# Two FNet and attention layers on one core: a PSUM bank closed to early maxima, an earlier root, query low parts on VectorE, and maxima paced by deadlines

## The chip, the cores and the metric

The kernel runs on one core of one Trainium2 chip. The metric is the device time of one execution in microseconds (us), the median of several runs. The core's engines work side by side and wait for each other by semaphores: TensorE (PE in the profile; its weight loads are PEld), VectorE (DVE), ScalarE (ACT), GpSimd (POOL), and SyncE (SP), which here only issues DMAs. PE writes its results into PSUM, which has eight banks of 128 partitions x 512 fp32 numbers.

## The reference, cut to what matters

Two different sublayers follow each other twice, on x of 2048 tokens x 512 features:

```
x = x + Real(DFT_seq(DFT_hidden(layernorm(x))))         # A: matrix products with cos and sin
x = x + softmax(q k^T / 4) v @ wo, of layernorm(x)      # B: 32 heads of 16, one k and one v for all heads
```

All of it is fp32. Layer norm has no weights; its epsilon is 1e-5. q is layernorm(x) @ wq, and k and v, 16 columns each, are shared by the heads.

## The kernel before

**Numbers in two parts.** Where one fp32r product would not be precise enough, an operand is split into a high part (rounded to fp32r) and a low part (what is left), and a product is made of three matmuls (`mm3`, lines 86 to 89). So most steps of preparation are a copy to the high part on ScalarE and a subtraction for the low part on VectorE or GpSimd (`split_ps`, `split_sb`, `split_act`, lines 70 to 84).

**Two layers, two phases each.** `phase_a` (line 733) makes the Fourier sublayer and the queries, keys and values; `phase_b` (line 1132) makes the attention and its output projection. Tokens are 16 tiles of 128, in four blocks (`tb`) of four tiles.

**Phase A** is a loop over n = 0 to 127: four blocks x (cosine, sine) x 16 tiles of the sequence. One n multiplies one 128x512 piece of the sequence matrix (loaded as `craw`, split into `ch` and `cl`) with the normalised input (`xnh`, `xnl`). From n = 48 on, `z_rows` (line 800) runs two matmuls at a time, on the upper and lower 64 rows of the array, and takes two pieces together. After each block, the hidden matrix follows (`y_tile`, `y_rows`), the residual is added and stored to `mid` by a DMA from GpSimd's queue, and the tile gets its layer norm: statistics on VectorE (`ln_stats`), the square root on ScalarE and the variance plus epsilon on GpSimd (`ln_root`, line 146), a reciprocal and four small operations (`ln_inv`, line 153), and the normalisation itself, in place (`ln_apply`, line 190). Then it is transposed on PE into PSUM bank z and split (`tr_tile`, line 263); from it come keys and values (`kv`) and queries (`q_mm`, `q_half`, `q_rows`). Query parts go to DRAM (`q_store`, `q_half_store`), 6 DMAs on SP for each group of heads.

**Maxima.** The softmax needs the maximum of each row of scores before phase B exponentiates it. For each unit (query tile, pair of heads, half of the array, quarter of the keys), PE multiplies queries and keys into a PSUM bank and VectorE reduces 512 numbers to their maximum. Some of these (`EARLY`, lines 35 to 40) run in phase A, between other matmuls: `pump` (line 445) offers a turn after each pair of matmuls, and `issue` (line 453) takes it if a bank is free by the planner's own clocks (`clk`: it adds 0.6 us to VectorE for each maximum, and keeps the times at which the three y banks and the one z bank come free). It picks bank z if that is free no later than the next y bank, and if `hold` isn't set. The others are listed in `units` (line 945), 1472 a layer, and run in phase B.

**PSUM.** Three banks y and one bank z, one at a time by turns, and two pairs x of two banks. Bank z serves the transposes (line 266), the early maxima, and in phase B the sum of the attention.

**The tail of phase A.** The last block's tiles 12 to 15 come late, and each is handled on its own. Tiles 12 and 13 are finished at n = 119; then, at the end of the n named, root of both (119), `ln_inv` (120), normalisation of 12 (121), transposes of 12 and normalisation of 13 (122), transposes of 13 (123), keys and values of both (124). After the loop (lines 915 to 942) an order written out by hand follows: `y_tile` of 14 and 15, transposes of 14 (`tr(14)`), the first two query groups of tiles 12 and 13 (`q_half(12, 0)`, `q_half(12, 1)`) with the root of tile 15 between them, their stores, the third group, `tr(15)`, the fourth, keys and values of 14 and 15, the queries of 14 and 15 by `q_rows`, the last maxima of tile 0, the row maxima written into the query tile (`max_rows_pe`, line 547), and six units as a lead for phase B. `q_split` (line 366) copies a query group twice on ScalarE (`raw`, then the high part), and GpSimd subtracts for the low part; for groups 2 and 3 of tiles 14 and 15 this is deferred (`st["subs"]`) to after `max_rows_pe`. `raw` is one tile, used for groups 0 and 1 and again for 2 and 3.

**Phase B** is a loop over n = 0 to 511: 16 query tiles x 32 steps. A step has four score matmuls (`score`, line 963), exponentials of 128x1024 on ScalarE, four matmuls with the values (`pv`, line 987) for the step two before, and maxima of later query tiles (`more_max`), up to two after the second score and two after the fourth. How many is set by `owed`:

```
return min(3 * (n + 1) + 6, len(units)) - o.done
```

A query tile's maxima must be done 8 steps before it starts (`max_neg_a`, with an assertion at lines 1177 to 1181; the two halves of the last two tiles have dates of their own). The order of the two halves of the array in a step follows the unit that is next (`g`, line 1148).

Of the kernel before, what the change touches and what calls it, by code (L numbers as in the profile page):

```python
# [22 lines left out]
NT = S // P  # L23
# [6 lines left out]
NSTEP = 32  # L30
# [17 lines left out]
def fnet_mqa_kernel(ctx: ExitStack, tc: tile.TileContext, x_in, ct, dt_, wq, wkv, wo, out):  # L48
# [6 lines left out]
    def f(ap):  # L55
        return ap.bitcast(F32)
# [139 lines left out]
    def make_layer(L, src, mid, dst, last):  # L196
# [169 lines left out]
        def q_split(t0, g, pq):  # L366
            if g == 0:
                st["raw"] = half(6)
                if t0 == 14:
                    st["stage"] = slot(3, F32R)  # L370
            hl = half((4, 5, 0, 1)[g], F32R) if t0 == 12 else st["stage"][:, g * 512:(g + 1) * 512]
            raw = st["raw"][:, 256 * (g % 2):256 * (g % 2) + 256]
            nc.scalar.copy(raw, pq)
            nc.scalar.copy(hl[:, :256], raw)
            st["qs", t0, g] = hl
            sub = lambda: nc.gpsimd.tensor_sub(hl[:, 256:], raw, f(hl[:, :256]))
            (st["subs"].append(sub) if t0 == 14 and g > 1 else sub())

        def q_half_store(t0, g):
            hl = st["qs", t0, g]  # L380
# [352 lines left out]
        def phase_a(extra):  # L733
# [111 lines left out]
            add(120, lambda: ln_inv(*st["root"]))  # L845
            add(121, lambda: apply(12))
            add(122, lambda: (tr(12), apply(13)))
            add(123, lambda: tr(13))
            add(124, kv_early)
            for k in ((125, 1), (125, 3), (126, 0), (126, 1), (126, 3), (127, 0), (127, 1), (127, 3)):  # L850
                inner[k] = [lambda: take(ma, 1)]
# [2 lines left out]
            for n in range(128):  # L854
# [47 lines left out]
                if n % 32 == 31 and tb < 3:  # L902
# [5 lines left out]
                    for k, v in prep_tasks(tb, dict(x1)).items():  # L908
                        for fn in v:
                            if isinstance(k, tuple):  # L910
                                inner.setdefault(k, []).append(fn)
                            else:
# [5 lines left out]
            y_tile(3, 3, zh, zl, x1[3], {2: [lambda: root(14, 1)], 4: [lambda: ln_inv(*st["root"], nc.vector)],  # L918
                                         6: [lambda: apply(14)]})
            tr(14)  # L920
            q_half(12, 0, *xt[0])
            root(15, 1)
            ln_inv(*st["root"], nc.vector)
            apply(15)
            q_half(12, 1, *xt[0])
            q_half_store(12, 0)
            q_half(12, 2, *xt[0])
            q_half_store(12, 1)
# [7 lines left out]
            take(mb, 99)  # L936
            max_neg(0, 0, HALF, 5)
            max_rows_pe(0, 0, HALF)
            for sub in st["subs"]:
                sub()  # L940
            for k in range(6):
                more_max()

# [8 lines left out]
                max_half(*units[o.done])  # L952
                o.done += 1

        def owed(n):
            return min(3 * (n + 1) + 6, len(units)) - o.done

        def done_with(i, pr):
            return all(u[:2] > (i, pr) for u in units[o.done:])
# [172 lines left out]
        def phase_b(nxt):  # L1132
            nonlocal woh, wol, osp
            woh = slot(4, F32R).rearrange("p (k e) -> p k e", k=NK)
            wol = slot(5, F32R).rearrange("p (k e) -> p k e", k=NK)
            def wo_load(j):
                st["wo", j] = half(4 + j)
                nc.sync.dma_start(st["wo", j], wo[:, j, :])

            behind = []  # L1140
            for n in range(NT * NSTEP):
                i, s_ = divmod(n, NSTEP)
                if len(behind) == 2:
                    pv(*behind.pop(0))
                behind.append((i, s_))
                if i > 0 and s_ == 13:
                    o_proj(i - 1)
                g = units[o.done][2] if o.done < len(units) else 1
                for j, m in ((g, 0), (1 - g, 2), (2 + g, 0), (3 - g, 2)):
                    score(i, s_, j)  # L1150
                    for _ in range(m):
                        if owed(n) >= 1:
                            more_max()
                if n in (1, 3):
                    q_half_store(12, 2 + n // 2)
                if i == 0 and 17 <= s_ <= 23 and s_ % 2:
                    q_half_store(14, s_ // 2 - 8)
                if 12 <= n < 16:
                    wo_load(n - 12)
                if n == 25:  # L1160
                    osp = slot(3, F32R).rearrange("p (a h n) -> p a h n", a=2, h=2)
                if i == 0 and s_ in (20, 22, 24, 26):
                    j = s_ // 2 - 10
                    split_sb(st["wo", j], woh[:, j, :], wol[:, j, :], nc.gpsimd)
                if i > 0:
                    for fn in out_tasks(i - 1).get(s_, ()):
                        fn()
                for j in range(2, NT):
                    if i == (j // 4 if j < 5 else j - 4 if j < 13 else j - 2):
                        at = {2: 11, 3: 27, 4: 6}.get(j, 0)  # L1170
                        if s_ == at:
                            qT_load(j)
                        if s_ == at + 4:
                            o.loaded.add(j)
                for fn in half_tasks(i).get(s_, ()):
                    fn()
                for at, j, p0, np_ in ((NT - AHEAD, i, HALF, HALF), (NSTEP - AHEAD, i + 1, 0, HALF if i >= NT - 3 else NPAIR)):
                    if j in (0, NT - 2, NT - 1) or j == i + 1 < NT:
                        if s_ == at:
                            assert done_with(j, p0 + np_ - 1)  # L1180
                            max_neg_a(j, p0, np_)
                        if s_ == at + 1:
                            max_neg_b(np_)
                        if s_ == at + 2:
                            max_rows(j, p0, np_)
            if nxt is not None:
                nxt.a_start()
            for at in behind:
                pv(*at)
            return {**out_tasks(NT - 1), 12: [lambda: o_proj(NT - 1)]}  # L1190
# [65 lines left out]
```

## Time and profile before

| | us |
|---|---|
| median of 3 runs | 3546.07 (3544.29 to 3546.45) |
| the profiled execution | 3549.72 |
| its span, first to last instruction | 3547.9 |
| PE busy | 3505.9 (99%) |
| DVE busy | 2714.7 (77%) |
| ACT busy | 2503.3 (71%) |
| POOL busy | 830.5 (23%) |

The profile is of one execution. A line of its timeline has a start and a duration in us, the engine, the line of the kernel, the operation, the names of the tiles written and read, shapes, how many instructions were merged into it (x2), and in brackets the idle time of the engine before it and what ended it. A line of a group has busy time and mean ns of one, then idle time. A line of the windows view has the stretch and its length, the busy time of PE, PEld, DVE, ACT and POOL (each with its count of instructions), then the clock granted to PE as a share of the full one, the share of DMA, and GB/s. Matmuls are pipelined, so a matmul's duration is longer than the time from one to the next. Layer 0 starts phase B near 632 us, layer 1 near 2393 us.

### The profile page before, as it was taken

How to read it: one execution, taken by the hardware profiler on the slowest of the kernel's cores; microseconds unless marked ns; L12 is line 12 of the kernel's file. 1: busy time of each engine (PE TensorE's matmuls, PEld its weight loads, DVE VectorE, ACT ScalarE, POOL GpSimd, SP SyncE). 2: the span in 40 equal slices, each digit the busy share in tenths (PEclk: the TensorE clock that was granted, in tenths of full speed). 3: DMA queues.
4: the chain of work that ended last, by engine and by line, in shares of the span. 5: the costliest groups of instructions: out<-in, count | busy, mean ns of one | idle time of the engine just before them, and what ended most of it. 6: DMA issues, size and time to landing. Idle time of an engine off the chain costs nothing.

```text
span 3547.9 us, 64282 instructions
## 1 busy us (share of the span) xinstructions
PE 3505.9 (99%) x24576; PEld 1874.8 (53%) x24576; DVE 2714.7 (77%) x4892; ACT 2503.3 (71%) x3210; POOL 830.5 (23%) x1262
## 2 busy tenths in 40 slices
PE   8999999999999999999999999999999999999999
PEld 6887878433333333333378878883333333333333
DVE  6267776888888888888432777768888888888883
ACT  4223733888888888888932247438888888888888
POOL 4244342211221122112213443422101110111011
PEclk9999999999999999999999999999999999999999
DMA  6435252311111100111144342523111111011100
GB/s 191 150 144 167 80 165 87 85 56 34 35 35 51 36 23 23 49 34 26 40 137 128 127 150 90 153 66 88 47 37 35 49 34 38 23 35 37 37 23 25
DMA packets 224900, 254.55 MB, mean 72 GB/s; under 512 B 52880, under 2 KB 174800, under 8 KB 217424
## 3 DMA queue, kind: packets, MB, share of 16 engines
q1 hardware_dynamic: 210384, 233.12, 21.6%
q0 software_dynamic: 14208, 17.33, 1.6%
q8 instruction: 193, 3.16, 0.4%
q14 instruction: 115, 0.94, 0.1%
HBM read 187.16 MB, written 65.27 MB: 71 GB/s over the span
## 4 chain that ended last, share of the span: by engine, by line
PE 91%; issue 2%; DVE 2%; ACT 2%; POOL 1%; DMA 1%; SPq 0%; ACTq 0%; POOLq 0%; DVEq 0%
PE z L994 29%; PE x L980 19%; PE y L408 13%; PE x L809 11%; PE y L87 3%; PE y L88 3%; PE y L89 2%; PE y L475 2%; PE x L87 2%; PE x L89 2%; PE x L88 2%; PE x L593 1%; PE z L475 1%; DVE row L191 1%; POOL cl L79 1%
## 5 line engine op out<-in xcount | busy, mean ns | idle before, releaser
L983 ACT ACTIVATE slot<-x 128x1024 f32<-128x1024 f32 x2000 | 1945.9, 1024 | 284.5 <-PE x L980 276.2
L409 DVE TENSOR_REDUCE mxp<-y 128x1 f32<-128x512 f32 x2944 | 1849.6, 684 | 181.5 <-PE y L408 168.7
L994 PE MATMUL z<-slot,v 128*32 128x512 f32 x8192 | 1096.3, 605 | 1.6 <-DVE lnv L1105 0.7
L980 PE MATMUL x<-slot,kz 64*128 64x512 f32 x2976 | 677.3, 450 | 2.2 <-DMA slot<-craw 1.7
L980 PEld LDWEIGHTS x<-slot,kz 64*128 64x128 f32 x2976 | 279.2, 184 | 744.7 <-ACT slot L983 685.8
L408 PE MATMUL y<-kz,slot 64*128 64x512 f32 x2176 | 581.6, 397 | 1.9 <-DVE mxp L409 1.9
L809 PE MATMUL x<-cl,xnh 64*128 64x512 f32 (+1 forms) x1536 | 355.8, 357 | 0.0
L994 PEld LDWEIGHTS z<-slot,v 128*32 128x32 f32 x8192 | 163.4, 108 | 363.7 <-issue 332.8
L809 PE MATMUL x<-ch,xnh 64*128 64x512 f32 (+1 forms) x1536 | 348.1, 361 | 2.3 <-ACT row L796 2.2
L809 PE MATMUL x<-ch,xnl 64*128 64x512 f32 (+1 forms) x1536 | 346.2, 362 | 0.9 <-ACT xnl L580 0.9
L408 PEld LDWEIGHTS y<-kz,slot 64*128 64x128 f32 x2176 | 276.7, 186 | 22.8 <-DVE mxp L409 10.8
L79 POOL TENSOR_TENSOR cl<-craw,ch 128x512 fp32r<-128x512 f32 x176 | 223.9, 1295 | 225.5 <-ACT ch L78 174.3
L78 ACT CAST ch<-craw 128x512 fp32r<-128x512 f32 x256 | 154.6, 622 | 170.9 <-PE x L89 87.1
L475 PE MATMUL y<-kz,slot 64*128 64x512 f32 x690 | 271.7, 405 | 2.1 <-ACT rel L479 1.2
L543 POOL DMA_DIRECT2D slot<-mt x224 | 112.1, 508 | 585.2 <-PE y L408 490.1
L809 PEld LDWEIGHTS x<-ch,xnh 64*128 64x128 f32 x1536 | 213.1, 188 | 23.3 <-issue 5.2
L809 PEld LDWEIGHTS x<-cl,xnh 64*128 64x128 f32 x1536 | 217.7, 188 | 12.6
L489 DVE TENSOR_REDUCE mxe<-y 128x1 f32<-128x512 f32 x316 | 198.8, 679 | 29.3 <-PE y L475 28.7
L809 PEld LDWEIGHTS x<-ch,xnl 64*128 64x128 f32 x1536 | 209.7, 187 | 21.1 <-issue 5.9
L1035 POOL TENSOR_TENSOR row<-row,row 128x256 f32<-128x256 f32 x63 | 46.5, 738 | 700.3 <-DMA row<-rd 654.0
L87 PE MATMUL x<-ch,xnh 128*128 128x512 f32 x384 | 154.3, 402 | 9.1 <-ACT ch L78 8.4
L89 PE MATMUL x<-ch,xnl 128*128 128x512 f32 x384 | 153.4, 399 | 2.6 <-POOL xnl L659 2.6
(198 smaller groups left out, 4143.3 us busy)
## 6 DMA issues: line engine op xcount, KB each, us to landing
craw<-ct_in SPq DMA_DIRECT2D x112, 512.0 KB
slot<-qd SPq DMA_DIRECT2D x44, 1024.0 KB
qd<-row SPq DMA_DIRECT2D x144, 128.0 KB
od<-row SPq DMA_DIRECT2D x252, 64.0 KB
row<-wqd SPq DMA_DIRECT2D x48, 256.0 KB
row<-x_in SPq DMA_DIRECT2D x32, 256.0 KB
mid<-row POOLq DMA_DIRECT2D x32, 256.0 KB, 2.4
craw<-ct_in SPq DMA_DIRECT2D x32, 256.0 KB
```

Of the source, the lines that this page charges most:

```text
L79: (eng or nc.vector).tensor_sub(lo, raw, f(hi))
L87: nc.tensor.matmul(ps_, ah, bh, start=start, stop=False)
L88: nc.tensor.matmul(ps_, ah, bl, start=False, stop=False)
L89: nc.tensor.matmul(ps_, al, bh, start=False, stop=stop)
L408: nc.tensor.matmul(pm, o.qT[i][gs, pr, :], kz[gs, c0:c0 + n], start=True, stop=True)
L409: nc.vector.reduce_max(to, pm, axis=AX.X)
L475: nc.tensor.matmul(pm, o.qT[i][gs, pr, :], k[gs, c0:c0 + 512], start=True, stop=True)
L489: nc.vector.reduce_max(to, pm, axis=AX.X)
L809: nc.tensor.matmul(z[d], a[gs, s, d * P:(d + 1) * P], b[gs, :], start=first and q < 2 and e == 0, stop=last and q > 1 and e == len(turns) - 1)
L980: nc.tensor.matmul(st["e"][:, g, :], kz[64 * g:64 * g + KR, c * P:(c + 1) * P], o.qT[i][64 * g:64 * g + KR, cp:cp + 4, :], start=True, sto ...
L983: nc.scalar.activation(ptiles[i, s_][:, 2 * w:2 * w + 2, :], st.pop("e"), AF.Exp, scale=DH ** -0.5)
L994: nc.tensor.matmul(a[32 * j:32 * j + 32, :], v1[:, c, :], pt[:, j, :], start=c == 0, stop=c == NT - 1)
```

## The change

Four edits, all in the order of work; no arithmetic is changed.

1. **Bank z closed to maxima.** `hold` is set after the second quarter of n = 122, that is ahead of the transposes of tile 12, and released behind those of tile 13. In between, early maxima use y banks only.
2. **The last tile's root sooner.** `root(15, 1)` stands ahead of `q_half(12, 0)` instead of behind it.
3. **First query low parts by VectorE.** The subtractions for groups 0 and 1 of tiles 12 and 13 are deferred and run on VectorE (`lows(2)`), behind `q_half(12, 1)` and tile 15's normalisation, ahead of the first store. The deferred ones of tiles 14 and 15 stay on GpSimd where they were.
4. **Maxima per step by deadlines.** `owed` gives way to `share`: each date at which a set of units must be done is a goal; a step gets the largest of (units still missing) / (steps left) over the goals, at least 2, with the fraction carried over, at most 4.

```diff
-            sub = lambda: nc.gpsimd.tensor_sub(hl[:, 256:], raw, f(hl[:, :256]))
-            (st["subs"].append(sub) if t0 == 14 and g > 1 else sub())
+            sub = lambda eng=nc.gpsimd: eng.tensor_sub(hl[:, 256:], raw, f(hl[:, :256]))
+            (st["subs"].append(sub) if (t0 == 14) == (g > 1) else sub())
+
+        def lows(n, eng=nc.vector):
+            for _ in range(n):
+                st["subs"].pop(0)(eng)
...
-            add(123, lambda: tr(13))
+            add(123, lambda: (tr(13), st.update(hold=False)))
+            inner[122, 1] = [lambda: st.update(hold=True)]
...
             tr(14)
+            root(15, 1)
             q_half(12, 0, *xt[0])
-            root(15, 1)
             ln_inv(*st["root"], nc.vector)
             apply(15)
             q_half(12, 1, *xt[0])
+            lows(2)
             q_half_store(12, 0)
...
-            for sub in st["subs"]:
-                sub()
+            lows(2, nc.gpsimd)
...
-        def owed(n):
-            return min(3 * (n + 1) + 6, len(units)) - o.done
+        goals = []
+        for j in range(NT):
+            for lim in (HALF, NPAIR):
+                at = NSTEP * (j - 1) + NSTEP - AHEAD if j < NT - 2 or lim == HALF else NSTEP * j + NT - AHEAD
+                if j == 0:
+                    at = NT - AHEAD
+                goals.append((sum(u[0] < j or (u[0] == j and u[1] < lim) for u in units), at))
+
+        def share(n):
+            need = max((c - o.done) / max(1, at - n) for c, at in goals if at > n or c > o.done)
+            st["due"] = min(st.get("due", 0.0) + max(2.0, need), 4.0)
+            k = int(st["due"])
+            st["due"] -= k
+            return k
...
+                left = share(n) if o.done < len(units) else 0
                 for j, m in ((g, 0), (1 - g, 2), (2 + g, 0), (3 - g, 2)):
                     score(i, s_, j)
                     for _ in range(m):
-                        if owed(n) >= 1:
+                        if left:
                             more_max()
+                            left -= 1
```

## The prediction

> **What bounds the kernel now.** I read the chain that ended last first, then the timeline of each engine at the places where TensorE (PE) is idle or slow, then the granted clock around them.
>
> ```profile
> PE 91%; issue 2%; DVE 2%; ACT 2%; POOL 1%; DMA 1%; SPq 0%; ACTq 0%; POOLq 0%; DVEq 0%
> ```
>
> PE makes up 91% of the chain. So a change pays where PE stands idle, or where it runs at less than its full clock; other engines' time counts only where PE waits for it. The longest stage is phase B (512 steps in each layer). Its maxima on VectorE (DVE) show its beat, here in layer 1:
>
> ```profile
> 2408.70 1.89 DVE L409 TENSOR_REDUCE mxp<-y 128x1 f32<-128x512 f32 x3 [0.24 <-PE y L408]
> 2410.84 1.89 DVE L409 TENSOR_REDUCE mxp<-y 128x1 f32<-128x512 f32 x3 [0.24 <-PE y L408]
> 2412.96 1.89 DVE L409 TENSOR_REDUCE mxp<-y 128x1 f32<-128x512 f32 x3 [0.24 <-PE y L408]
> ```
>
> Three maxima a step, a step each 2.12 to 2.14 us (from start to start), and DVE waits 0.24 us of each for PE. The end of phase A is where PE stops. Its own timeline, first layer 0, then the same place in layer 1:
>
> ```profile
> 582.32 0.50 PE L475 MATMUL z<-kz,slot 64*128 64x512 f32 x1
> ...
> 583.37 0.49 PE L475 MATMUL y<-kz,slot 64*128 64x512 f32 x1
> ...
> 584.51 0.30 PE L809 MATMUL x<-ch,xnl 64*128 64x256 f32 x2
> 584.63 0.30 PE L809 MATMUL x<-cl,xnh 64*128 64x256 f32 x2
> ...
> 584.77 0.48 PE L809 MATMUL x<-ch,xnh 64*128 64x256 f32 x2
> 586.96 0.66 PE L268 MATMUL z<-ident,row 128*128 128x128 f32 x4 [1.70 <-DVE mxp L489]
> ```
>
> ```profile
> 2347.97 0.66 PE L268 MATMUL z<-ident,row 128*128 128x128 f32 x4 [1.71 <-DVE mxp L489]
> ```
>
> The transposes of tile 13 (L268) want bank z, and wait 1.7 us in each layer for a maximum that was put into that bank ahead of them. DVE at that time:
>
> ```profile
> 581.57 0.69 DVE L75 TENSOR_TENSOR xnl<-z,xnh 128x512 fp32r<-128x512 f32 x1 [0.65 <-ACT xnh L71]
> ...
> 582.63 1.28 DVE L489 TENSOR_REDUCE mxp<-y 128x1 f32<-128x512 f32 x2
> 583.83 0.68 DVE L489 TENSOR_REDUCE mxp<-z 128x1 f32<-128x512 f32 x1
> 584.43 1.88 DVE L489 TENSOR_REDUCE mxp<-y 128x1 f32<-128x512 f32 x3
> 586.22 0.68 DVE L489 TENSOR_REDUCE mxp<-z 128x1 f32<-128x512 f32 x1
> ```
>
> Seven maxima are served one after another, 0.6 us each; the last, in z, ends at 586.90. What follows is worse than it looks. In the windows view the column that counts is PEclk, the granted clock:
>
> ```profile
> 584.50:587.90 3.40, 1.70 (x20) 1.21 (x18) 2.40 (x5) 0.25 (x1) 0.00 (x0) 1.00 0.00 0
> 587.90:591.40 3.50, 3.50 (x36) 3.50 (x34) 1.89 (x3) 1.57 (x4) 2.52 (x2) 0.51 0.02 5
> ...
> 2349.20:2352.60 3.40, 3.40 (x36) 3.40 (x34) 1.89 (x3) 1.28 (x4) 2.52 (x2) 0.50 0.00 0
> 301.20:304.60 3.40, 2.42 (x16) 1.34 (x14) 2.55 (x5) 1.21 (x4) 0.09 (x1) 1.00 0.00 0
> 304.60:308.00 3.40, 3.40 (x10) 2.62 (x9) 1.69 (x3) 0.00 (x0) 0.00 (x0) 0.50 0.00 0
> 2062.50:2065.90 3.40, 2.43 (x12) 1.77 (x13) 2.72 (x5) 1.09 (x4) 0.00 (x0) 1.00 0.02 5
> 2065.90:2069.30 3.40, 3.40 (x25) 2.54 (x25) 1.77 (x4) 1.22 (x2) 0.50 (x1) 1.00 0.33 93
> ```
>
> Behind the stall PE runs 3.4 us at half clock, in both layers. The matmul pairs there:
>
> ```profile
> 588.25 0.42 PE L809 MATMUL x<-ch,xnl 64*128 64x256 f32 x2
> 588.47 0.42 PE L809 MATMUL x<-ch,xnh 64*128 64x256 f32 x2
> ```
>
> From one pair to the next it is 0.22 us; from 584.51 to 584.63 it was 0.12. At half clock 3.4 us do the work of about 1.85: the dip costs some 1.55 us, which is to say nearly as much as the stall itself.
>
> **The change, part by part.** *Bank z closed (hold), each layer.* No operation is added or removed: the planner puts the maxima between the two tiles' transposes into the three y banks alone. Gone is the wait at 586.96 (1.70). Gone too is a wait of 0.2 us at 582.32, where the first of these z maxima waited for the DVE subtraction that read z until 582.26. What is late next is a y bank: the max at 583.37 reuses the bank of the first one, whose reduction ended just before, at 583.3. With hold it would come one max sooner in the order but at the same planner time, that is 0.2 us ahead of that reduction, as the wait at z no longer delays it: 0.2 us given back. From there DVE serves one in 0.6 us and the planner counts 0.6 (line 431), so no bank is later than planned. Net 1.70, between 0.85 (half of it returns as waits at y) and 1.85 (from 586.96 back to 585.11, one pair behind the last). One max slides behind tile 13's transposes; there PE has the same work, and DVE was idle for it. Tile 13's subtraction is needed only by the key matmul, 24 pairs or 2.8 us later.
>
> *The dip.* Without the stall, PE has no idle time here that could bring the dip on: 1.55 more, or nothing if something else causes it. As the windows need not lie alike in every execution (0.98 us of idle time brought a dip at 304.60 and 0.97 none at 2065.90), I count nine in ten: 1.4.
>
> The Trainium skill, "TensorE: Matmul & The Clock Gate" (Part 1: The HAM clock gate), says that the array clock halves by a free-running window of 3413 ns and, under HAM oscillation, warns of idle gaps above some 3.4 us. The dips' length here agrees (3.4 us in the windows view). By the gap length that it names, 1.7 us is too short to be the cause, and the sum would lose the 1.4. The dip at 304.60, behind 0.98 us of idle time, speaks against that reading.
>
> *Last tile's root sooner, low parts by VectorE, each layer.* The rows of tile 15:
>
> ```profile
> 616.62 0.37 ACT L373 COPY row<-x 128x256 f32<-128x256 f32 x1 [0.82 <-PE x L89]
> ...
> 617.33 0.29 ACT L149 ACTIVATE lnw<-mv,eps 128x1 f32<-128x1 f32 x1
> ...
> 619.90 0.41 ACT L374 CAST row<-row 128x256 fp32r<-128x256 f32 x1
> 620.75 0.60 ACT L71 ACTIVATE xnh<-z 128x512 fp32r<-128x512 f32 x1 [0.44 <-PE z L268]
> ```
>
> ```profile
> 615.75 0.60 POOL L577 DMA_DIRECT2D mid<-row  x1 [4.48 <-DVE row L576]
> 617.51 0.73 POOL L376 TENSOR_TENSOR row<-row,row 128x256 fp32r<-128x256 f32 x1 [1.16 <-ACT row L374]
> ```
>
> ```profile
> 616.22 0.18 DVE L144 BATCH_NORM_AGGREGATE mv<-bst 128x2 f32<-128x6 f32 x1
> ...
> 617.85 0.41 DVE L157 TENSOR_TENSOR lnw<-rs 128x1 f32<-128x1 f32 x1
> ...
> 619.05 0.88 DVE L191 TENSOR_SCALAR row<-row,mv,rs 128x512 f32<-128x512 f32 x1
> ...
> L73 DVE SCALAR_TENSOR_TENSOR slot<-x,slot 128x256 fp32r<-128x256 f32 x16 | 6.7, 420 | 4.4 <-ACT slot L71 4.4
> ```
>
> ```profile
> 620.08 0.63 PE L268 MATMUL z<-ident,row 128*128 128x128 f32 x4 [0.68 <-DVE row L191]
> ...
> 622.12 0.38 PE L88 MATMUL y<-xnl,wkvh 128*128 128x256 f32 x1
> ```
>
> The root stood behind the first query copies on ScalarE (616.62 to 617.4) and its chain beside a GpSimd subtraction, which stretched L157 to 0.41 us. Moved ahead, it starts when the variance is there (L144, 616.40), and with 0.29 for the root, tile 14's subtraction before it on DVE until 617.0 and five small DVE operations of 0.2 each (L157 has 0.41 only beside GpSimd) it ends near 618.0. The normalisation (L191) writes in place, so it must also wait until the store issued by GpSimd at 615.75 has landed; the page's section 6 has 2.4 us for these:
>
> ```profile
> mid<-row POOLq DMA_DIRECT2D x32, 256.0 KB, 2.4
> ```
>
> So L191 starts near 618.2 and, at 0.55 to 0.88, ends at 619.1 at the latest, and PE, done with the matmuls ahead at 619.2, can transpose then instead of at 620.08: 0.84 us. Not all of it lasts. ScalarE must still finish L374 (619.90 + 0.41), so tile 15's high part ends near 620.85 instead of 621.35, its low part 0.5 us sooner than before, and the key matmul that reads it (622.12) starts at 621.58: net 0.54. The two low parts on DVE (a subtraction of 128x256, which the trace does not show on DVE from SBUF alone; between the 0.42 of L73, as wide, and the 0.69 of L75, twice as wide; I take 0.42) lie between L191 and tile 15's own subtraction near 620.85, where DVE is otherwise idle. At 0.69, and with L191 ending last, the first would end at 619.8, and the ScalarE copy that overwrites its raw part, due at 619.5 (ahead of the L374 at 619.90), would wait 0.3 us. Queued behind the first of their stores on SP are the other query stores, nothing else for long:
>
> ```profile
> 617.45 7.86 SPq L385 DMA_DIRECT2D qd<-row  x12
> 633.93 1.58 SPq L556 DMA_DIRECT2D slot<-craw  x2
> ```
>
> The stores end 8.6 us before SP's next turn, so 1 us later costs nothing. The term: 0.54, between 0.2 (that wait, or GpSimd's next subtraction stretching tile 15's low part by 0.33 as the one at 617.51 did L157 and the one after it L191) and 0.84.
>
> *Maxima per step by deadlines.* There are 1472 units in a layer, 6 done beforehand. Before, three a step until step 488. The deadlines ask (1472 - 6) / 488 = 3.004 a step, the tightest of all (the next, step 408, asks 2.97); the loads keep ahead of both. Worked through, it is three in every step but 192 and 379, which get four, and none after 487. DVE needs 4 x 0.63 = 2.5 us for such a step, 0.4 over the beat, and makes it good in two steps of 0.24 idle: I cost it at nothing, at most 4 x 0.4 = 1.6 in all.
>
> *Sum.* 1.70 + 1.40 + 0.54 = 3.64 a layer, 7.3 in all. The profiled execution took 3549.72 us (span 3547.9), 3.65 above the median; the same 7.3 taken from the median 3546.07 gives **3538.8**. A measurement of this kernel can tell about 0.2%, 7.1 us, from no change: the forecast lies on that line (3539.0).
>
> **The rivals.** *The wait moves to the y banks.* Three banks for seven maxima instead of four; for it, the max at 583.37 already found its bank free only just in time; against it, DVE and planner keep one pace. Half the stall returns: 2 x (0.85 + 0.54) = 2.8 with the dip kept, 5.6 without: 3540.5 to 3543.3.
>
> *The dip is not the stall's.* For it, 2062.50 lost as much as 301.20 without a dip; against it, both layers have it right behind the stall. 2 x (1.70 + 0.54) = 4.5: 3541.6. The Trainium skill's page, read by its gap length, would have it so.
>
> *A dip fewer elsewhere*, as everything shifts against the windows: 1.6 less, 3537.2.
>
> *The change does not do it*: something else ends the wait, and only the root counts, 1.1: 3545.0. The row names the maximum, so this is small.
>
> *Slower.* Place: phase B. The extra max at step 192 swaps which half of the array each step starts with, until 379: 187 steps a layer, 374 in all. It decides from 7.3 / 374 = 0.02 us a step; at 0.05 it costs 18.7, and gives 3557.5. Against it, successive steps already start with opposite halves, and the rows above lie 2.14 and 2.12 apart.
>
> **How the numbers follow.** Forecast (3537.4 to 3540.4): 0.62, of which 0.47 lies below 3539.0. Wait moved to y: 0.17. Dip not the stall's: 0.08. A dip fewer elsewhere: 0.06. Without effect: 0.03. Slower: 0.04, of which 0.01 stays within 0.2%. Faster by over 0.2%: 0.47 + 0.06 = 0.53; slower 0.03; the rest, 0.44, within. The range 3536.5 to 3543.0 holds the forecast, the dip rivals and nearly all of the y-bank case, over 0.8.
>
> **What would show it.** Right: no idle time above 0.3 us before the L268 of tile 13, all maxima between the two tiles in y, a granted clock of 1.00 behind it in both layers, L268 of tile 15 without a wait, the phase B beat unchanged at 2.13. Wrong: PE idle before L475 on y by DVE L489; a dip that stays; a beat above 2.15 between steps 192 and 379; ScalarE late at tile 15 by the low parts.

## The result and the profile after

| | before | after |
|---|---|---|
| median of 22 runs each (range), us | 3547.39 (3544.29 to 3550.55) | 3542.59 (3540.58 to 3544.26) |
| ratio, 95% interval | | 0.9986 (0.998 to 0.9991) |
| profiled execution, us (span) | 3549.72 (3547.9) | 3541.5 (3539.7) |

The kernel is faster by about 4.8 us, between 3.2 and 7.1 us by the interval. That lies within the 0.2% named in the prediction, for which it gave the smaller chance (0.44). The forecast was 3538.8 and 7.3 us of gain, so two thirds of the gain came. The time lies in the wide range of 3536.5 to 3543.0, but not in the forecast's own part of it, 3537.4 to 3540.4. It lies where the prediction put two of its rivals (3540.5 to 3543.3 and 3541.6), so it is the traces that have to tell them apart. The kernel before was itself 1.3 us slower in these runs than the 3546.07 that the forecast started from.

The chain that ended last, from the page of the kernel after, has PE at 93% where it had 91%:

```profile
PE 93%; DVE 2%; ACT 2%; issue 2%; POOL 1%; DMA 1%; SPq 0%; ACTq 0%; DVEq 0%; POOLq 0%
```

PE's timeline of the kernel after, at the end of phase A, layer 0 and then layer 1 (start, us, engine, line, operation; a wait would stand in brackets at the end):

```profile
578.10 0.66 PE L268 MATMUL z<-ident,row 128*128 128x128 f32 x4
...
580.29 0.39 PE L479 MATMUL y<-kz,slot 64*128 64x512 f32 x1
...
582.60 0.40 PE L479 MATMUL y<-kz,slot 64*128 64x512 f32 x1
582.92 0.66 PE L268 MATMUL z<-ident,row 128*128 128x128 f32 x4
...
2336.13 0.66 PE L268 MATMUL z<-ident,row 128*128 128x128 f32 x4
2340.95 0.66 PE L268 MATMUL z<-ident,row 128*128 128x128 f32 x4
```

Six maxima stand between the two tiles, where seven stood, all of them in y, and the transposes of tile 13 start without a wait, 4.82 us behind those of tile 12 in both layers. The same distance was 6.71 us (580.25 to 586.96). The granted clock around it, from the windows view of the kernel after (stretch; length, PE, PEld, DVE, ACT, POOL busy; PEclk; DMA share; GB/s):

```profile
579.80:583.20 3.40, 3.33 (x44) 2.88 (x41) 3.40 (x7) 0.00 (x0) 0.00 (x0) 1.00 0.01 2
583.20:586.60 3.40, 3.40 (x53) 3.23 (x52) 3.31 (x6) 1.82 (x4) 1.80 (x2) 1.00 0.02 5
2341.30:2344.70 3.40, 3.40 (x53) 3.23 (x52) 3.31 (x6) 1.82 (x4) 1.87 (x2) 1.00 0.00 0
```

PE is busy nearly throughout (3.33 us of the first 3.40) and the clock is 1.00 in both layers: stall and dip are gone. DVE is now busy nearly all the time as well, up to 3.40 of 3.40 us.

**Tile 15** came out differently in the two layers. VectorE, ScalarE and PE of the kernel after, first layer 0 and then layer 1:

```profile
613.51 0.55 DVE L191 TENSOR_SCALAR row<-row,mv,rs 128x512 f32<-128x512 f32 x1 [0.97 <-DMA mid<-row]
613.97 0.75 DVE L376 TENSOR_TENSOR row<-row,row 128x256 fp32r<-128x256 f32 x2
...
2370.92 0.55 DVE L191 TENSOR_SCALAR row<-row,mv,rs 128x512 f32<-128x512 f32 x1 [0.36 <-DMA mid<-row]
2371.38 0.76 DVE L376 TENSOR_TENSOR row<-row,row 128x256 fp32r<-128x256 f32 x2
```

```profile
614.48 0.37 ACT L373 COPY row<-x 128x256 f32<-128x256 f32 x1 [0.99 <-DVE row L376]
...
2372.13 0.37 ACT L373 COPY row<-x 128x256 f32<-128x256 f32 x1 [0.60 <-PE x L89]
```

```profile
609.21 0.60 PE L268 MATMUL z<-ident,row 128*128 128x128 f32 x4
614.20 0.63 PE L268 MATMUL z<-ident,row 128*128 128x128 f32 x4
635.16 1.93 PE L1011 MATMUL z<-slot,v 128*32 128x512 f32 x8
...
2367.24 0.60 PE L268 MATMUL z<-ident,row 128*128 128x128 f32 x4
2392.79 1.93 PE L1011 MATMUL z<-slot,v 128*32 128x512 f32 x8
```

Tile 15's normalisation (L191) no longer waits for the root but for the store of the row that it overwrites, 0.97 us in layer 0 and 0.36 in layer 1. The two low parts (L376) stand behind it. In layer 0 the third query copy on ScalarE (L373) therefore waits for a low part; in layer 1 it waits for PE, as it should. The transposes of tile 15 come 4.99 us behind those of tile 14 in layer 0 and 4.68 in layer 1; before it was 5.52 in both. From tile 14's transposes to the first matmul with values it is now 25.95 and 25.55 us, where it was 26.16 and 26.12: 0.21 and 0.57 gained. The two ends of that way in the kernel before, layer 0:

```profile
614.56 0.60 PE L268 MATMUL z<-ident,row 128*128 128x128 f32 x4
640.72 1.93 PE L994 MATMUL z<-slot,v 128*32 128x512 f32 x8
```

The way also depends on when the half clock at the start of phase B sets in. In layer 1 of the run of edit 1 it set in later than usual, and the way was 25.83 us without any edit to tile 15.

### The profile page after: what moved, and what is told of

It is laid out like the page before. It is cut to its first block, busy times and chain, and to the rows that moved or that the text cites. A ratio compares the mean times of both kernels' runs of the same rounds, so it can differ in the third digit from the quotient of the medians.

```text
span 3539.7 us, 64288 instructions
## 1 busy us (share of the span) xinstructions
PE 3502.0 (99%) x24576; PEld 1870.9 (53%) x24576; DVE 2713.8 (77%) x4896; ACT 2502.3 (71%) x3210; POOL 825.9 (23%) x1258
## 4 chain that ended last, share of the span: by engine, by line
PE 93%; DVE 2%; ACT 2%; issue 2%; POOL 1%; DMA 1%; SPq 0%; ACTq 0%; DVEq 0%; POOLq 0%
PE z L1011 29%; PE x L997 19%; PE y L412 13%; PE x L813 11%; PE y L87 3%; PE y L479 3%; PE y L88 3%; PE y L89 2%; PE x L87 2%; PE x L89 2%; PE x L88 2%; PE x L597 2%; PE z L479 1%; DVE row L191 1%; POOL cl L79 0%
```

## The experiments

The theory at the start: hold, and the dip that goes with the stall, make the gain, and the shortfall against 7.3 us is a dip that the stall does not bring on in every execution (theory A in the quoted texts; A' and A'' are its versions for tile 15 and for the pacing). The rival, theory B: hold and dip are worth what was forecast, the dip in nine of ten, and root, low parts or the new pacing give some back. A third reading is that the stall has nothing to do with the dip. Four runs take the change apart; the rest follow their leads, and the theory of the dip was changed on the way. Each expectation is quoted as it was written before its run.

**Edit 1 alone.** `hold` in the kernel before:

```diff
-            add(123, lambda: tr(13))
+            add(123, lambda: (tr(13), st.update(hold=False)))
+            inner[122, 1] = [lambda: st.update(hold=True)]
```

> Edit 1 alone (bank z closed to maxima between the transposes of tiles 12 and 13). Theory A (stall always, half-clock dip only in executions whose clock window holds most of the stall, about one in two): 1.8 us of stall in each layer, and 1.57 in half of the cases: 5.2 us faster than before. Theory B (the recorded forecast: dip in nine of ten): 2 x (1.7 + 1.4) = 6.2 faster. If the wait only moved to the y banks: under 3 us faster. In the trace: no idle time above 0.3 us before L268 of tile 13, six maxima between the two tiles' transposes instead of seven.

Measured: 3542.36 us against 3547.18 for the kernel before, ratio 0.9988 (0.9979 to 0.9997). Tile 13 follows tile 12 after 4.82 us in both layers, with six maxima between them, and there is no dip. The gain of 4.3 us (1.1 to 7.5) is about that of the whole change; it does not part the expected 5.2 from 6.2, nor from less than 3.

**The stall kept, its idle time filled.** Seven matmuls whose result is not used stand ahead of tile 13's transposes in the kernel before:

```diff
+            def fill():
+                pm = bank("y")
+                for _ in range(7):
+                    nc.tensor.matmul(pm, o.qT[0][:, 0, :], kz[:, :512], start=True, stop=True)
-            add(123, lambda: tr(13))
+            add(123, lambda: (fill(), tr(13)))
```

> Kernel before with seven full-array matmuls (0.23 us each, into a free y bank, their result not used) put ahead of tile 13's transposes: TensorE still cannot start those before the maximum in bank z is done, but it is not idle meanwhile. If the dip is the stall's: granted clock 1.00 behind it in both layers, while L268 of tile 13 stays near 586.9 after an unshifted start. Time: theory A 1.6 us faster than before (two layers, one in two), theory B 2.8 faster. If the dip is not caused by the idle time: the dip stays and the time is that of before.

PE's timeline in this kernel, then its windows, layer 0 and layer 1:

```profile
585.61 1.90 PE L851 MATMUL y<-kz,slot 128*128 128x512 f32 x7
587.38 0.66 PE L268 MATMUL z<-ident,row 128*128 128x128 f32 x4
...
2341.86 0.66 PE L268 MATMUL z<-ident,row 128*128 128x128 f32 x4
2348.57 0.66 PE L268 MATMUL z<-ident,row 128*128 128x128 f32 x4
```

```profile
584.50:588.00 3.50, 3.50 (x31) 2.55 (x27) 2.83 (x5) 0.00 (x0) 0.00 (x0) 1.00 0.00 0
588.00:591.40 3.40, 3.40 (x53) 3.27 (x53) 1.89 (x3) 1.98 (x5) 2.14 (x2) 1.00 0.02 5
...
2349.00:2352.40 3.40, 3.40 (x54) 3.11 (x51) 1.89 (x3) 1.83 (x4) 1.95 (x2) 1.00 0.02 5
```

Tile 13 still comes 6.71 us behind tile 12, so the stall costs what it did. But PE is busy in it, and the clock stays at 1.00 in both layers. The dip belongs to the idle time. In time the run is not told from the kernel before: 3545.61 us, 0.9996 (0.9987 to 1.0005). The two dips alone are worth some 3 us, which lies in that interval, and this execution had half-clock windows at six other places of phase A. Layer 1 also shows that a store can land late in the old order: tile 15's normalisation waited 0.90 us for it, and its transposes came 6.04 us behind tile 14's, not 5.52.

**Edits 2 and 3 alone** (root and low parts, as in the change, in the kernel before):

```diff
+            root(15, 1)
             q_half(12, 0, *xt[0])
-            root(15, 1)
...
             q_half(12, 1, *xt[0])
+            lows(2)
```

> Edits 2 and 3 alone (root of tile 15 sooner, first two low parts on VectorE). Recorded forecast: 0.54 us a layer, 1.1 faster. Theory A': 0.2 a layer, 0.4 faster, because the ScalarE copy of the third query group waits for the first low part, which stands on VectorE behind tile 15's normalisation, which waits for the store of tile 15: the copy starts 0.7 us behind the third group's last matmul instead of 0.4. Behind the stall of tile 13, which stays, the trace shows a dip in each layer by theory B; by theory A in about one of two.

Measured: 3548.19 us, 1.0001 (0.9993 to 1.001). The values' first matmul comes 25.81 and 25.55 us behind tile 14's transposes, 0.35 and 0.57 sooner: real, but too little to show in a time. This execution holds the best pair of windows of the study, as both layers keep the stall:

```profile
582.40:585.80 3.40, 1.70 (x24) 1.38 (x23) 3.26 (x6) 0.00 (x0) 0.00 (x0) 1.00 0.00 0
585.80:589.20 3.40, 3.40 (x52) 3.23 (x54) 1.89 (x3) 1.83 (x4) 1.61 (x2) 1.00 0.03 5
...
2340.30:2343.70 3.40, 1.69 (x21) 1.20 (x19) 2.46 (x5) 0.19 (x1) 0.00 (x0) 0.99 0.00 0
2343.70:2347.10 3.40, 3.40 (x34) 3.40 (x32) 1.89 (x3) 1.63 (x4) 2.41 (x2) 0.50 0.00 0
```

The same 1.7 us of PE in each 3.4 us, in one layer followed by half clock and in the other not. The halved stretches of an execution begin and end on one grid, with a line every 3.41 us. In layer 0 the stall began 1.62 us behind a line, in layer 1 at 0.86. So the amount of idle time alone does not decide. (In the run with the filled stall, the 1.7 us ahead of tile 13's transposes begin 0.84 and 0.74 us behind a line, near the place that dips here; so its clock was not kept by a lucky place.)

**Edit 4 alone** (`share` in place of `owed`, as in the change).

> Edit 4 alone (maxima per step by deadlines). Recorded forecast: no change. Theory A'': each of the two steps with four maxima costs 0.6 to 0.8 us in both layers, and the end gives back 1.3 (step 488 has no maxima left): 0.4 a layer, 0.8 us slower. If the swapped order of the halves between steps 192 and 379 cost something, the beat there would be above that of before. The stall of tile 13 stays; its dips as in the run before this one: each layer by theory B, one in two by A.

Measured: 3549.55 us, 1.0005 (0.9996 to 1.0013): no gain, and a loss of some 1.8 us at the middle that the interval does not tell from nothing. Where it could lie is seen at a step with four maxima. DVE and PE of the kernel after, around step 192 of layer 0:

```profile
1058.36 1.89 DVE L413 TENSOR_REDUCE mxp<-y 128x1 f32<-128x512 f32 x3 [0.24 <-PE y L412]
1060.48 2.48 DVE L413 TENSOR_REDUCE mxp<-y 128x1 f32<-128x512 f32 x4 [0.24 <-PE y L412]
```

```profile
1058.72 1.06 PE L1011 MATMUL z<-slot,v 128*32 128x512 f32 x8
1061.65 1.07 PE L1011 MATMUL z<-slot,v 128*32 128x512 f32 x8
1063.77 1.06 PE L1011 MATMUL z<-slot,v 128*32 128x512 f32 x8
```

PE takes 2.93 us for this step instead of 2.12, and the next ones take 2.12 again: 0.81 us, not 0.4, and no step catches it up. The end of phase B gives most of it back: in layer 0 of the kernel before, a step among the last maxima takes 2.93 us (1725.38 to 1728.31), and the step at its place in the kernel after takes 1.66 (1721.43 to 1723.09). From first to last matmul with values, phase B took 1137.0 us on average in the layers with `share` (six, 1136.4 to 1137.4) and 1136.6 in the layers of the nine profiles with three maxima a step and nothing filled in at its start (eighteen, 1135.0 to 1137.5): some 0.3 us a layer, less than the spread. The mean step between 200 and 370, tile changes included, is 2.25 us with and without it, so the swapped order of the halves costs nothing.

The stall stands in both layers again, with a dip behind it in layer 1 alone; in layer 0 it began 2.16 us behind a line of the grid.

**Four and two maxima by turns**, a single run, in the kernel before. It takes the price of an uneven step by itself, 244 pairs in a layer:

```diff
-            return min(3 * (n + 1) + 6, len(units)) - o.done
+            return min(6 * (n // 2) + (6 if n % 2 else 4) + 6, len(units)) - o.done
```

> Kernel before with four and two maxima in turn instead of three in each step: the doubled form of what edit 4 does twice a layer. If the extra maximum only moves work (a step with four 0.7 us longer, one with two as much shorter), the time is that of before within 10 us and a pair of steps takes 4.25 us. If each step with four loses 0.4 us that is not given back, 244 of them in each layer cost 195 us. The stall of tile 13 stays: two more samples, as in the run before this one.

Measured: 3814.91 us, 267 above the kernel before. PE's timeline of it shows the pair:

```profile
701.01 1.06 PE L994 MATMUL z<-slot,v 128*32 128x512 f32 x8
702.89 1.06 PE L994 MATMUL z<-slot,v 128*32 128x512 f32 x8
705.83 1.06 PE L994 MATMUL z<-slot,v 128*32 128x512 f32 x8
```

The step with two takes 1.88 us, the one with four 2.94: 4.82 a pair instead of 4.25. The 0.57 us lost, over 2 x 244 pairs, would make 278, near the 267. A step with fewer maxima is quicker by 0.24 us only, so most of what a full step loses does not come back in the next one. (With an even number of maxima a step, each step also starts with the same half of the array. A step of four is no longer for it: 2.94 us here, 2.93 in the kernel after.)

**The first low part ahead of the normalisation.** From the kernel after, with `owed` put back:

```diff
             ln_inv(*st["root"], nc.vector)
+            lows(1)
             apply(15)
             q_half(12, 1, *xt[0])
-            lows(2)
+            lows(1)
```

> Edits 1, 2 and 3 without edit 4, and the first low part put on VectorE ahead of tile 15's normalisation, into the 1 us that this waits for the store to land; the second stays behind. If the ScalarE copy of the third query group waits for the first low part (theory A'), it now starts 0.4 us behind that group's last matmul instead of 0.7, and the stretch from tile 14's transposes to the first matmul with the values loses 0.55 us against the kernel before in both layers, not 0.2 to 0.6. If the copy waits for something else, it stays at 0.7. Time: 2 x (1.6 + 0.5) = 4.2 faster than before in every execution, and about 1.4 more on the mean for the dips: 5.6; by the recorded forecast 7.3.

VectorE and ScalarE of it, layer 0:

```profile
614.54 0.42 DVE L376 TENSOR_TENSOR row<-row,row 128x256 fp32r<-128x256 f32 x1
615.36 0.55 DVE L191 TENSOR_SCALAR row<-row,mv,rs 128x512 f32<-128x512 f32 x1 [0.40 <-DMA mid<-row]
```

```profile
616.08 0.37 ACT L373 COPY row<-x 128x256 f32<-128x256 f32 x1 [0.60 <-PE x L89]
```

The copy waits for PE again, the wait for the store is 0.40, and the values' first matmul comes at 25.58 and 25.56 us in both layers. That settles layer 0's missing 0.3 us: the low parts behind a late L191. The store landed nearly as late in layer 0 of this run as in the runs with both low parts behind L191 (L191 starts 4.16 us behind tile 14's transposes here, 4.12 to 4.30 there). In time it is like the change: 3542.93 us, 0.9984 (0.9975 to 0.9993).

**Edit 2 alone**, the low parts left to GpSimd, a single run:

```diff
+            root(15, 1)
             q_half(12, 0, *xt[0])
-            root(15, 1)
```

> Edit 2 alone (root of tile 15 sooner, all low parts on GpSimd as before). The copy of the third query group does not wait (0.4 us behind the last matmul), but GpSimd's second subtraction lies beside tile 15's normalisation and stretches it to some 0.9 us: tile 15's transposes 0.4 us sooner than before instead of 0.84, and the whole stretch 0.3 to 0.5. The stall of tile 13 stays: two more samples of where it lies in the clock's window. Theory A: a dip behind it if it starts within some 0 to 1.2 us of a window's start, none if it starts at 1.6 or later. Theory B: a dip in each.

Measured: 3546.32 us. The values' first matmul comes at 25.61 and 25.59, the whole 0.55 in both layers. The normalisation was not stretched to 0.9 us, as expected, but took 0.55. The root makes the gain; moving the low parts to VectorE adds nothing, and in layer 0 of the change it takes some away.

**Before twice more and after once more**, unchanged, a single run each, to see whether dips and stretches repeat.

> Kernel before once more, for its profile: two more samples of the stall of tile 13. Theory A: a dip behind it if it starts within some 0 to 1.2 us of a clock window's start, none if it starts at 1.6 or later; over all samples about one in two. Theory B: a dip in each.

> The kernel before a third time, for its profile: the stall of 1.7 us ahead of tile 13's transposes in both layers, and a dip behind it where the stall starts 0.3 to 0.9 us into a clock window (ten of ten so far), none where it starts at 1.6 or later (none of two so far). By theory A about one of two, by theory B nine of ten.

> The changed kernel once more, for its profile: no idle time above 0.3 us and no half clock behind tile 13's transposes in either layer; elsewhere 5 to 7 windows at half clock (four of them at the starts of phase B). Tile 15: in a layer where the store lands late (the normalisation waits over 0.8 us for it) the third group's copy starts 0.6 to 0.7 us behind its last matmul, otherwise 0.04.

Measured: 3547.77, 3546.27 and 3541.72 us. Both of before dip behind the stall in both layers, after in neither.

Over the kernels so far that keep the stall idle there are fourteen such places (two layers in seven profiles): twelve dip, two do not. In the six profiles in which PE does not stand idle there, none of twelve places dips (one of the six is of the last run told below).

Two other waits of phase A, of 2.2 us near 281 and of 0.98 us near 302, can be put on the grid in the same way. With the stall that makes forty cases, and the middle of the wait sorts them: at 1.2 to 2.05 us behind a line, half clock followed 26 times out of 26; elsewhere (0.9 to 1.0, or from 2.26 on), twice out of 14. The text of the next run, quoted below, says 0 of 14. But the wait near 281 was followed by half clock in the run of edit 2 alone, with its middle at 0.98, and in the run with the filled stall, with its middle at 0.92. The first of these, on the lines of its grid:

```profile
281.26:284.67 3.41, 1.35 (x10) 1.09 (x12) 3.41 (x4) 0.65 (x2) 1.62 (x2) 1.00 0.91 304
284.67:288.08 3.41, 3.41 (x18) 2.42 (x14) 2.78 (x6) 1.80 (x3) 2.77 (x3) 0.50 0.33 81
```

In the same two executions the wait of 0.98 us near 302, with its middle at 0.92 and 1.01, did not dip. So the middle does not sort waits of different lengths there. What sorts all forty is whether PE is idle during the whole of 1.57 to 1.88 us behind a line: 28 of 28 that are, dip, and 0 of 12 that are not. Either rule was found in data already at hand, so it needed a run of its own.

**The stall moved on the grid.** Five matmuls whose result is not used, well ahead of the stall, in the kernel before:

```diff
+            def shift():
+                pm = bank("y")
+                for _ in range(5):
+                    nc.tensor.matmul(pm, xnh[:, 0, :P], xnh[:, 1, :], start=True, stop=True)
+
+            add(119, shift)
             add(119, y_early)
```

> The kernel before with five full-array matmuls, whose result is not used, ahead of the block's y tiles at n = 119, in both layers: about 1.3 us of PE work well before the stall. They move the stall against the clock's grid of 3.41 us and leave its length as it is (tile 13's transposes 6.71 us behind tile 12's, 1.7 us of it idle). Theory, from the profiles so far: waits near 281 and 302 us and this stall, all of 0.98 to 2.2 us, were followed by half clock whenever their middle lay 1.2 to 2.05 us behind a line of the grid (26 of 26), and never when it lay elsewhere (0 of 14). By it, each layer dips if and only if the middle of its stall lies in that part; in layer 0, where the stall began 0.33 to 0.92 us behind a line in most profiles, it should begin at 1.6 to 2.3, with its middle at 2.5 to 3.1, and not dip. In layer 1 the shift comes on top of what layer 0 and the start of phase B did to the position, so it is read from the trace. Rival: the idle time alone brings the dip on, by chance, 12 times in 14, so both layers dip again wherever the stall lies. Time: 2 x 1.3 more PE work, less 1.6 for each dip that is gone: within 3 us of before's 3547, not to be told apart in one look.

Its windows, layer 0 and layer 1, each the stall and what follows:

```profile
584.55:587.95 3.40, 1.73 (x20) 1.27 (x18) 2.79 (x5) 0.00 (x0) 0.00 (x0) 1.00 0.00 0
587.95:591.35 3.40, 3.40 (x52) 3.25 (x52) 1.89 (x3) 1.91 (x5) 2.08 (x2) 1.00 0.02 5
2344.40:2347.80 3.40, 1.70 (x22) 1.21 (x18) 2.75 (x5) 0.00 (x0) 0.00 (x0) 1.00 0.00 0
2347.80:2351.20 3.40, 3.40 (x31) 3.40 (x32) 1.89 (x3) 1.63 (x4) 2.12 (x2) 0.50 0.00 0
```

The stall is as long as before in both layers (6.71 us from tile to tile). In layer 0 it began 2.64 us behind a line, later than the 1.6 to 2.3 that were expected, with its middle at 3.5: no dip. In layer 1 it began at 1.13, its middle at 2.0: a dip. The waits near 281 (middle at 3.2, none) and 302 (1.8, dip) fit as well, and both rules give all four. The two stalls alone would not rule chance out: at 12 in 14, just one of two dips in about one case of four. With the forty waits before them, chance is no longer likely, and the position on the grid is what sorts the cases. In time, 3548.67 us in a single run, nothing is told apart, as expected.

The positions also say why the stall so often dips in layer 0. In five of the seven profiles the wait near 302 had dipped, and in four of these nothing else halved the clock on the way to the stall, which then begins 282.9 us later: 82.9 times 3.413, so that it lies 0.3 to 0.5 us earlier on the grid, in the part that dips. One dip sets up the next. For layer 1 this was not worked out.

**The start of phase B filled as well.** In every other profile phase B begins with 3.4 or 6.8 us at half clock in each layer. Nine matmuls whose result is not used go between the six maxima there, in the kernel with the first low part ahead:

```diff
             for k in range(6):
                 more_max()
+                pm = bank("z") if k in (1, 3, 4, 5) else None
+                for _ in range((0, 3, 0, 1, 1, 4)[k]):
+                    nc.tensor.matmul(pm, xnh[:, 0, :P], xnh[:, 1, :], start=True, stop=True)
```

> The kernel of edits 1 to 3 with the first low part moved ahead, and nine full-array matmuls of 0.23 us (into bank z, their result not used) put into the idle time of TensorE at the start of phase B, where each layer has two windows at half clock (6.8 us). If idle time inside a clock window is what brings half clock on, these windows go in both layers and each costs some 1.4 us: up to 5 us faster than the same kernel without them, about 3538. If the start of phase B is bound by the exponentials and the row maxima's DMAs whatever the clock, the clock is full and the time the same. If the filling matmuls hold up the scores, 1 to 2 us slower.

The windows at that place, first of the kernel after, then of this one:

```profile
627.00:630.40 3.40, 1.96 (x6) 0.79 (x6) 2.98 (x5) 2.57 (x6) 1.75 (x3) 1.00 0.02 3
630.40:633.80 3.40, 2.78 (x11) 1.76 (x11) 2.53 (x5) 1.78 (x2) 1.24 (x5) 0.50 0.39 79
633.80:637.20 3.40, 3.40 (x17) 0.87 (x15) 2.03 (x4) 2.08 (x3) 0.00 (x0) 0.50 0.48 96
```

```profile
627.20:630.60 3.40, 3.38 (x11) 1.68 (x11) 2.62 (x5) 2.90 (x6) 1.39 (x3) 1.00 0.02 2
630.60:634.00 3.40, 2.95 (x15) 1.66 (x15) 2.27 (x4) 1.22 (x2) 1.62 (x5) 1.00 0.32 65
634.00:637.40 3.40, 3.40 (x22) 1.49 (x22) 2.86 (x6) 2.98 (x4) 0.00 (x0) 1.00 0.51 104
```

The first stretch is filled from 1.96 to 3.38 us, and the two behind it run at full clock. Measured: 3538.7 us, 0.9977 (0.9968 to 0.9986) against the kernel before, the lowest median of the study. Its own base, the kernel with the first low part ahead, had 0.9984 (0.9975 to 0.9993), so the filling is worth some 2.5 us at the middle, half of the "up to 5". That interval and the change's (0.998 to 0.9991) both overlap with this one, so the lead is likely rather than shown.

## Why the prediction came out as it did

In the traces the mechanism is right: stall and dip are gone in both layers, and tile 15 comes sooner. The time fell into the wide range on the side of less gain, outside the forecast's own part. It is in the range only because the range was wide enough to hold the rivals as well. The two that are near the measured time fall by the traces: PE does not wait for a y bank between tiles 12 and 13, and the dip went with the idle time. By its steps:

- **Hold: forecast 1.70 a layer, measured 1.59.** 1.89 us went between the transposes of tiles 12 and 13, and 0.3 came back behind tile 13: from there to tile 14 it takes 26.3 us with 19 maxima on the way, where it takes 26.0 with 18 in the layers that do not dip and have no hold. The prediction let one maximum slide there for nothing ("there PE has the same work"), but with it that way is 0.3 us longer. The wait did not move to the y banks.
- **Dip: forecast 1.40, measured 1.37 in the profiles.** With a dip the way from tile 13 to tile 14 takes 27.6 us, without it 26.0: 1.6 a dip, in 12 of 14 places. "Nine in ten" was right as a number for this place; behind it stands where the idle time falls on the grid, as far as the forty waits and the moved stall show. What the forecast took for granted, that a dip less here is a dip less in all, is in doubt by the timed runs (below). The rival by the gap length that the Trainium skill names ("TensorE: Matmul & The Clock Gate", Part 1: The HAM clock gate) falls: 1.7 us of idle time were enough, and filling them took the dip away. Its free-running window of 3413 ns agrees with the grid of 3.41 us.
- **Root: forecast 0.54, measured 0.57 in layer 1 and 0.21 in layer 0** (0.36 in the second profile of the kernel after). The step that failed is "L191 starts near 618.2", which took the page's 2.4 us for the landing of tile 15's store. That is 3.64 us behind tile 14's transposes (614.56 in that execution). In layer 1 it was 3.68 (2367.24 to 2370.92), but in layer 0 it was 4.30 (609.21 to 613.51), and 4.12 in the second profile: the store landed later, and the low parts behind L191 held the ScalarE copy. That is the wait which the prediction named for its lower end of 0.2.
- **Low parts on DVE: forecast 0.42, measured 0.42** alone.
- **Maxima by deadlines: forecast nothing, at most 0.4 for a step of four; measured 0.81 for such a step**, some 0.3 a layer by the end. The step that failed is "makes it good in two steps of 0.24 idle". DVE took 2.48 us for such a step, as forecast, but PE loses 0.81, and the steps behind keep their 2.12 us.

Together: 2 x 1.59 + 2 x 1.37 + (0.29 + 0.57) - 2 x 0.3 = 6.2 us, with 0.29 the mean of layer 0's two profiles. The profiled executions of the two kernels agree: before 3549.72, 3547.77 and 3546.27, mean 3547.9; after 3541.5 and 3541.72, mean 3541.6; difference 6.3. The timed medians say 4.8 (3.2 to 7.1), so the terms lie inside the interval and 1.4 us of the middle is unaccounted for.

A candidate for it is the rival that was priced in the other direction, a dip fewer elsewhere. Outside this place, the start of phase B and the last microseconds, the eight profiles with the idle stall hold 28 half-clock windows in all (3.5 each, 2 to 5), and the six without it hold 27 (4.5 each, 3 to 6). Layer 1's window near 2166 to 2172 is in all six of these and, at the same place of its layer, in five of the eight others. Since every microsecond that goes moves all that follows on the grid, other places may dip instead. One window more is 1.6 us. The two kernels' own profiles do not show it: 4, 4 and 2 such windows before, 3 and 4 after.

The timed runs say more, as each lists its granted clock. Its mean was 0.99570 over the 33 runs of the kernel before that were made beside edit 1, and 0.99586 over the 22 of the kernel after. A dip takes 0.0005 off it (half of 3.41 us in 3547), so 12/7 dips fewer would have added 0.0008. By this account half clock gave some 0.5 us of the gain and not 2.7, and the rest came from the waits and from tile 15. The run with the filled stall points the same way: 0.99609, about half of what two dips would add, and 1.4 us of gain at the middle where two dips would make some 3. So in the timed runs most of the half clock that went here came back elsewhere, or the kernel before had less of it than in its three profiles. The clocks are rounded to 0.001, about two windows, so this is a sign and not a count, and the cause of the shortfall stays open in part.

## What to carry to other kernels

A wait of 1.7 us on TensorE cost nearly twice its length here, so price a stall with the granted clock of the 3.4 us behind it. If the wait itself can't go, filling it with matmuls kept the clock here, and in one layer moving it by some 2 us did too. But count the half-clock windows of the whole execution, in several executions, before a dip that is gone at one place is booked as gain. An operation that overwrites its operand waited here until the store of the old contents had landed, so what stands behind it in the queue inherits the latest landing, not the median. And in a steady step with 0.24 us of slack, an extra unit cost 0.81 us, of which a lighter step gave back 0.24 only.

## What had not been expected of the hardware

- A wait of PE of 0.98 to 2.2 us was followed by 3.41 us at half clock when PE was idle during the whole of 1.57 to 1.88 us behind a line of the clock's grid (30 of 30 with the last run), and not otherwise (0 of 14). By the middle of the wait the rule is less sharp: 28 of 28 at 1.2 to 2.05 us, 2 of 16 elsewhere. This holds for three places of phase A and was read from the same cases. A wait of 0.99 us near 2062 dipped once with its middle at 2.8, waits of 0.8 us did not dip even where they covered that part, and several short waits at the start of phase B were followed by half clock too. So it is a rule of these places, and the mechanism behind it stays open.
- Half clock also came without any long wait. Ahead of the window near 2171 of the kernel before, PE waits five times between early maxima, for 0.2 us at most and 0.86 in all:

```profile
2168.31:2171.72 3.41, 2.55 (x12) 1.11 (x12) 3.18 (x11) 2.88 (x6) 0.00 (x0) 1.00 0.34 133
2171.72:2175.13 3.41, 3.41 (x18) 2.66 (x20) 2.12 (x7) 1.63 (x3) 0.00 (x0) 0.50 0.00 0
```

- The store of the same row came free later in layer 0 than in layer 1 in every execution with the earlier root in which L191 waited for it in both (4.12 to 4.30 us behind tile 14's transposes against 3.67 or 3.68, three profiles). Why is not known.
